# Sliding-window attention and a spectral mix on one core: attention by halves of the heads, mode weights by halves of the channels

## The chip, the core and the metric

The kernel runs on one core of a Trainium2 chip, as one launch. The metric is device time in microseconds from the launch's start to its end. The engines are PE (TensorE), DVE (VectorE), ACT (ScalarE), POOL (GpSimd) and SP (SyncE); the last two also issue the transfers here, POOL those that change the type from float32 to bfloat16 on the way, SP the others. Each engine takes its instructions in the order in which they stand in its queue.

## The reference

Attention with a causal window of 64 over 576 positions, for 8 batches and 8 heads of 64; the heads side by side are x (8 x 576 x 512). A real Fourier transform over the positions follows; of its frequencies the first 64 (the "modes") are each multiplied by a complex 512 x 512 matrix of their own, all others are set to zero; the inverse transform is added to x, and a dense layer with a ReLU is added to that.

```python
scores = scale * np.matmul(q, k.transpose(0, 1, 3, 2))
mask = (rel >= 0) & (rel < window)                    # window = 64
attn = softmax(where(mask, scores, -1e9)); x = heads side by side of (attn @ v)

X = np.fft.rfft(x, axis=1)
Xr, Xi = (np.real(X[:, :n_modes]), np.imag(X[:, :n_modes]))
Yr = np.einsum('bmd,mde->bme', Xr, w_r) - np.einsum('bmd,mde->bme', Xi, w_i)
Yi = np.einsum('bmd,mde->bme', Xr, w_i) + np.einsum('bmd,mde->bme', Xi, w_r)
Y[:, :n_modes] = Yr + 1j * Yi
u = x + np.fft.irfft(Y, n=S, axis=1)
return u + np.maximum(u @ w_ch, 0.0)
```

w_r and w_i are 64 matrices each of 512 x 512 float32, 1 MB a matrix, 134 MB in all. They are the bulk of what is read.

## The kernel before

**Attention** is written in 40 units (`units`), five for a batch: two for each half of the heads (4 heads, the positions 0 to 255 and 256 to 511), and one for the last 64 positions of both halves. A unit has 8 score tiles of 128 x 128 (the last 4): two heads of 64 rows by the 128 keys that the window can reach. One half of the heads of one batch is a group `g`; its q and k come as bfloat16 on 72 partitions (`load_qk`, POOL), its v as float32 (`load_v`, SP, rows of 256 bytes), which POOL casts (`cast_v`). `transpose_qk` turns q and k by 16 PE transposes and one ACT copy each, through the one PSUM bank of `ps_m`.

The order is written out by hand (`tc.manual_schedule()`), as a software pipeline over iterations `it`: for unit `it` PE subtracts the row maximum by a matmul (`do_sub`, L171) and ACT takes the exponential (`do_exp`, L179); for unit `it + 1` PE writes the mask and the scores (`do_s`, L144 to L158) and DVE takes the maximum (`do_max`, L165); for `it - 1` PE transposes the probabilities (`do_pt`, L186) and DVE copies them out (`do_ev`, L192); for `it - 2` PE multiplies by v (`do_pv`, L209) and DVE divides and writes `x_sb` (`do_norm`). The transposes of the next group stand between these. Once a batch is complete `do_dft` (L233) multiplies its x by the trigonometric table `trigF` in 20 matmuls into the bank of `ps_m`, and ACT copies the result into `XQ` (L235), with a negated copy of the imaginary part (L236). The columns of x that a DFT matmul takes are strided by four, so that the partition of `XQ` matches a load of the weights in which a partition reads four rows in one run of 8 KB.

Ahead of the loop come the masks and `trig_tables()`: a chain on DVE that ends in a Sin on ACT.

**The weights** come in 128 tiles (`wr` and `wi` of a mode) of 512 x 512, cast to bfloat16 by a POOL transfer (`load_weight`, L70), 512 KB each in SBUF, in a pool of 17. Seventeen are prefetched, spread over the 40 units. After attention the 64 modes follow in order: 8 matmuls of 16 columns x 512 for a mode (L404 and L406), a copy on ACT (L409), and two stores on SP (L410, L411) that gather the rows of `Yall`.

**The end**: the inverse table `trigI` is made (a chain of POOL, DVE and ACT, which the scheduler places into attention's last part); then for each batch and 128 positions one matmul gives the inverse transform (L425), DVE adds x (L428), PE transposes (L431), ACT copies (L435), four matmuls with `wch` follow (L438), and DVE and SP finish and store. The first of these matmuls needs all of `Yall`.

Of the kernel before, what the change touches and what calls it, by code (L numbers as in the profile page):

```python
# [13 lines left out]
ALU = mybir.AluOpType  # L14
# [3 lines left out]
W_BUFS = 17  # L18
# [6 lines left out]
def kernel(  # L25
# [15 lines left out]
    assert S == 576 and D == 64 and DM == 512 and H == 8  # L41
# [3 lines left out]
    NBLK = S // 64  # L45
    PSUM = bass.MemoryType.PSUM

    consts = ctx.enter_context(tc.tile_pool(name="consts", bufs=1))
# [10 lines left out]
    xpool = ctx.enter_context(tc.tile_pool(name="xpool", bufs=1))  # L59
    x_sb = xpool.tile([128, B, NTC, DM], BF16, name="x_sb")  # L60
    wch = xpool.tile([128, NDCH, DM], FP32R, name="wch")
    XQ = xpool.tile([128, NDCH, 3 * B, NM], BF16, name="XQ")
    Yall = xpool.tile([2 * NM, B, DM], BF16, name="Yall")
    wtpool = ctx.enter_context(tc.tile_pool(name="wtpool", bufs=W_BUFS))

    def load_weight(i):
        m, ri = divmod(i, 2)
        w = wtpool.tile([128, NDCH, DM], BF16, name="wi" if ri else "wr", tag="wt")
        src = moe_w_i if ri else moe_w_r
        nc.gpsimd.dma_start(out=w, in_=src[m].rearrange("(p c) e -> p c e", c=NDCH))  # L70
        return w

    wtiles = {}


    with ExitStack() as p1, tc.manual_schedule():
        rawp = p1.enter_context(tc.tile_pool(name="rawp", bufs=2))
        qtp = p1.enter_context(tc.tile_pool(name="qtp", bufs=3))
        vfp = p1.enter_context(tc.tile_pool(name="vfp", bufs=2))
        vdp = p1.enter_context(tc.tile_pool(name="vdp", bufs=1))  # L80
        ps_s = p1.enter_context(tc.tile_pool(name="ps_s", bufs=2, space=PSUM))
        ps_pt = p1.enter_context(tc.tile_pool(name="ps_pt", bufs=1, space=PSUM))
        ps_pv = p1.enter_context(tc.tile_pool(name="ps_pv", bufs=1, space=PSUM))
        ps_m = p1.enter_context(tc.tile_pool(name="ps_m", bufs=1, space=PSUM))

        NHB = 2 * B
        raws, qkT, vraw = {}, {}, {}

        def load_qk(g):
            b, hb = divmod(g, 2)  # L90
            for nm, src in (("k", k), ("q", q)):
                r = rawp.tile([72, 4, 8, D], BF16, name="raw" + nm, tag="raw" + nm)
                nc.gpsimd.dma_start(
                    out=r, in_=src[b, 4 * hb:4 * hb + 4].rearrange("h (p j) d -> p h j d", j=8))
                raws[g, nm] = r

        def load_v(g):
            b, hb = divmod(g, 2)
            vf = vfp.tile([128, NTC, 4, D], FP32, name="vf")
            vs = v[b, 4 * hb:4 * hb + 4]  # L100
            for c in range(4):
                nc.sync.dma_start(out=vf[:, c], in_=vs[:, c * 128:(c + 1) * 128, :].rearrange("h p d -> p h d"))
            nc.sync.dma_start(out=vf[0:64, 4], in_=vs[:, 512:576, :].rearrange("h p d -> p h d"))
            vraw[g] = vf
# [23 lines left out]
        for b in range(B):  # L128
            for hb in range(2):
                for cc in range(2):  # L130
                    tl = [(c2 * 4 + pr * 2 + par, 2 * b + hb, pr, 2 * (2 * cc + c2) + par)
                          for c2 in range(2) for pr in range(2) for par in range(2)]
                    units.append((b, hb, cc, tl))
            units.append((b, None, 2, [(hb * 2 + pr, 2 * b + hb, pr, 8) for hb in range(2) for pr in range(2)]))
        st = [dict() for _ in units]

        def do_s(u):
            b, hb, cc, tl = units[u]
            s = ps_s.tile([128, 8, 128], FP32, name="s")
            st[u]["s"] = s  # L140
            nb = len(tl) // 4
            for c2 in range(nb):
                mk = 2 if cc == 2 else (1 if (cc == 0 and c2 == 0) else 0)
                nc.tensor.matmul(out=s[:, 4 * c2:4 * c2 + 4, :], lhsT=ident_bf, rhs=mask_t[:, mk],  # L144
                                 start=True, stop=True)
            for t, g, pr, n in tl:
# [13 lines left out]

        def do_max(u):
            nt = len(units[u][3])
            mx = smp.tile([128, 8], FP32R, name="mx")
            st[u]["mx"] = mx
            nc.vector.tensor_reduce(out=mx[:, 0:nt], in_=st[u]["s"][:, 0:nt, :], axis=AX.X, op=ALU.max, negate=True)  # L165

        def do_sub(u):
            nt = len(units[u][3])
            s, mx = st[u]["s"], st[u]["mx"]
            for c2 in range(nt // 4):  # L170
                nc.tensor.matmul(out=s[:, 4 * c2:4 * c2 + 4, :], lhsT=ident_r,  # L171
                                 rhs=mx[:, 4 * c2:4 * c2 + 4].unsqueeze(2).to_broadcast([128, 4, 128]),
                                 start=False, stop=True, skip_group_check=True)

        def do_exp(u):
            nt = len(units[u][3])
            p = pp.tile([128, 8, 128], BF16, name="p")
            st[u]["p"] = p
            nc.scalar.activation(out=p[:, 0:nt, :], in_=st[u]["s"][:, 0:nt, :], func=ACT_F.Exp, scale=EX_SCALE)  # L179

        def do_pt(u):
            nt = len(units[u][3])
            pt = ps_pt.tile([128, 8, 128], BF16, name="pt")
            st[u]["pt"] = pt
            for t in range(nt):
                nc.tensor.transpose(out=pt[:, t, :], in_=st[u]["p"][:, t, :], identity=ident_bf)  # L186

        def do_ev(u):
            nt = len(units[u][3])
            ps = ptp.tile([128, 8, 128], BF16, name="pts")  # L190
            st[u]["ps"] = ps
            nc.vector.tensor_copy(out=ps[:, 0:nt, :], in_=st[u]["pt"][:, 0:nt, :])  # L192

        def do_pv(u):
            b, hb, cc, tl = units[u]
            o = ps_pv.tile([128, 2, 512], FP32, name="o")
            st[u]["o"] = o
            ps = st[u]["ps"]
            order = sorted(tl, key=lambda x: (x[0] // 4, x[2], x[3] % 2))
# [12 lines left out]

        def do_norm(u):
            b, hb, cc, tl = units[u]
            np_ = 128 if cc < 2 else 64
            o = st[u]["o"][0:np_, :, 0:260].rearrange("p c (h e) -> p c h e", e=65)
            r = smp.tile([128, 2, 4], FP32, name="r")
            nc.vector.reciprocal(out=r[0:np_].unsqueeze(3), in_=o[:, :, :, 64:65])
            rb = r[0:np_].unsqueeze(3).to_broadcast([np_, 2, 4, 64])
            if cc < 2:  # L220
                xo = x_sb[:, b, 2 * cc:2 * cc + 2, 256 * hb:256 * hb + 256]
                xo = xo.rearrange("p c (h d) -> p c h d", d=64)
            else:
                xo = x_sb[0:64, b, 4, :].rearrange("p (c h d) -> p c h d", c=2, d=64)
            nc.vector.tensor_tensor(out=xo, in0=o[:, :, :, 0:64], in1=rb, op=ALU.mult)  # L225
            st[u].clear()

        def do_dft(b):
            px = ps_m.tile([128, NDCH, 2 * NM], FP32, name="px", tag="misc")
            for dch in range(NDCH):  # L230
                for c in range(NTC):
                    nt = min(128, S - c * 128)
                    nc.tensor.matmul(out=px[:, dch, :], lhsT=x_sb[:nt, b, c, dch:DM:NDCH],  # L233
                                     rhs=trigF[:nt, c, :], start=(c == 0), stop=(c == NTC - 1))
            nc.scalar.copy(out=XQ[:, :, B + b:3 * B:B, :], in_=px.rearrange("p c (a m) -> p c a m", a=2))  # L235
            nc.scalar.mul(out=XQ[:, :, b, :], in_=px[:, :, NM:2 * NM], mul=-1.0)  # L236


        p0 = ExitStack()
        stmp = p0.enter_context(tc.tile_pool(name="stmp", bufs=1))  # L240
# [39 lines left out]
        nc.vector.tensor_copy(out=mask_t[:, 2, 1:4:2, :], in_=mask_t[:, 0, 0:4:2, :])  # L280

# [17 lines left out]
        p0.close()  # L299
        pp = p1.enter_context(tc.tile_pool(name="pp", bufs=2, reuse_waits="tile"))  # L300
        ptp = p1.enter_context(tc.tile_pool(name="ptp", bufs=2, reuse_waits="tile"))
        smp = p1.enter_context(tc.tile_pool(name="smp", bufs=3, reuse_waits="tile"))


        NU = len(units)

        def prep_for(u):

            b, hb, cc, tl = units[u]
            return 2 * b + hb if hb is not None and cc == 0 else None  # L310

        first = {}
        for u in range(NU):
            g = prep_for(u)
            if g is not None:
                first[g] = u

        tq = {}
        for g, u in first.items():
            grp = [("k", 0), ("q", 0), ("k", 1), ("q", 1)]  # L320
            for i, it in enumerate(grp):
                tq.setdefault(u - 3 + i // 2 if u else -3, []).append((g,) + it)
        npre = 0

        def prefetch(n):
            nonlocal npre
            for _ in range(n):
                if npre < W_BUFS:
                    wtiles[npre] = load_weight(npre)
                    npre += 1  # L330

        for it in range(-3, NU + 3):
# [3 lines left out]
            if 0 <= it < NU:  # L336
                do_sub(it)
                do_exp(it)
            if 0 <= it + 1 < NU:
                do_s(it + 1)  # L340
                do_max(it + 1)
            for x in todo[1:2]:
                transpose_qk(*x)
            if it >= 5 and it % 5 == 4:
                do_dft(it // 5 - 1)
            if 0 <= it - 1 < NU:
                do_pt(it - 1)
                do_ev(it - 1)
            if 0 <= it - 2 < NU:
                do_pv(it - 2)  # L350
                do_norm(it - 2)
# [3 lines left out]
            g = {u: g for g, u in first.items()}.get(it + 1)  # L355
            if g is not None and g + 2 < NHB:
                load_qk(g + 2)
                load_v(g + 2)
            if it >= 0:
                prefetch((it + 1) * W_BUFS // NU - npre)  # L360
            g = {u: g for g, u in first.items()}.get(it - 1)
            if g is not None and g + 1 < NHB:
                cast_v(g + 1)
            if it == 4:
# [110 lines left out]
```

## Time and profile before

| | |
|---|---|
| time, median of 3 runs | 555.59 us (554.82 to 560.37) |
| span of the profiled execution | 553.8 us |
| PE, DVE, ACT, POOL busy | 71%, 30%, 26%, 27% |
| share of the chain that ended last | DMA 53%, PE 32% |
| read from HBM, written | 163.58 MB, 9.44 MB |

The profiled execution's own time is its span and a little around it; the median of the runs lies 1.8 us above the span. A stretch's DMA share is the mean busy share of the 16 DMA engines, and goes above 1 where their packets overlap; its GB/s count what was written, for a casting load half of what was read. Busy PE time counts a matmul from start to modelled end, and matmuls overlap.

### The profile page before, as it was taken

The numbers are of one execution on the slowest core, as the hardware profiler recorded it, in microseconds if no ns is written. First come the engines' busy times: TensorE is split into PE (matmuls) and PEld (weight loads), VectorE is DVE, ScalarE is ACT, GpSimd is POOL, SyncE is SP. The second block draws the span as 40 slices with busy tenths as digits, with TensorE's granted clock in tenths as the row PEclk, the third lists the DMA queues.
The fourth block names the chain that finished last, engine by engine and source line by source line (L and its number), as shares of the span: only waits on it lengthen the run. The fifth ranks groups of instructions, "written<-read, shape, count | busy, mean of one in ns | idle before, by whom it ended". The sixth has DMA issues, their size and how long they took to land.

```text
span 553.8 us, 9433 instructions
## 1 busy us (share of the span) xinstructions
PE 391.0 (71%) x3896; PEld 207.8 (38%) x3896; DVE 168.3 (30%) x279; ACT 145.3 (26%) x222; POOL 150.0 (27%) x227
## 2 busy tenths in 40 slices
PE   0598899999997985556554655565475555699996
PEld 0366566666665441111111111121121111366664
DVE  5268176577569000000000000000000000287885
ACT  0465355556454130111011110111011011122221
POOL 7273474455532131222221222222121210000000
PEclk9999599999899798867788786778858888699999
DMA  9689999999964399999999999999999997034343
GB/s 155 103 144 228 163 161 200 191 180 206 176 130 78 55 216 215 214 214 215 214 215 214 215 214 215 214 215 213 214 215 214 214 214 155 7 139 143 133 138 129
DMA packets 77242, 98.14 MB, mean 177 GB/s; under 512 B 45456, under 2 KB 55696, under 8 KB 77200
## 3 DMA queue, kind: packets, MB, share of 16 engines
q0 software_dynamic: 31760, 77.62, 73.7%
q1 hardware_dynamic: 45440, 19.93, 15.0%
q8 instruction: 30, 0.49, 0.4%
q14 instruction: 12, 0.10, 0.1%
HBM read 163.58 MB, written 9.44 MB: 312 GB/s over the span
## 4 chain that ended last, share of the span: by engine, by line
DMA 53%; PE 32%; issue 6%; DVE 4%; POOL 3%; ACT 1%; SPq 0%; POOLq 0%; ACTq 0%
DMA wi<-in_moe_w_i_dram 48%; PE pout L438 7%; PE psut L431 4%; PE s L171 4%; PE px L233 3%; DVE mx L165 3%; DMA rawk<-in_k_dram 3%; PE tr L120 2%; PE s L144 2%; PE psy L425 2%; PE pt L186 2%; DMA vf<-in_v_dram 1%; PE o L209 1%; PE s L155 1%; PE s L152 1%
## 5 line engine op out<-in xcount | busy, mean ns | idle before, releaser
L406 PE MATMUL psm<-wi,XQ 128*16 128x512 bf16 x256 | 124.1, 486 | 99.2 <-DMA wi<-in_moe_w_i_dram 99.2
L404 PE MATMUL psm<-wr,XQ 128*16 128x512 bf16 x256 | 125.2, 490 | 20.0 <-DMA wr<-in_moe_w_r_dram 19.2
L428 DVE TENSOR_TENSOR ut<-x_sb,psy 128x512 f32<-128x512 bf16 (+1 forms) x40 | 27.1, 683 | 298.4 <-PE psy L425 297.0
L409 ACT CAST stg<-psm 16x512 bf16<-16x512 f32 x64 | 36.8, 575 | 253.5 <-PE psm L406 249.7
L404 PEld LDWEIGHTS <-XQ 128*16 128x16 bf16 x256 | 29.1, 114 | 191.6 <-issue 134.8
L70 POOL DMA_DIRECT2D wi<-in_moe_w_i_dram x64 | 34.2, 534 | 123.4 <-DMA wi<-in_moe_w_i_dram 94.3
L70 POOL DMA_DIRECT2D wr<-in_moe_w_r_dram x64 | 34.2, 535 | 102.2 <-DMA wr<-in_moe_w_r_dram 54.3
L165 DVE TENSOR_REDUCE mx<-s 128x8 fp32r<-128x1024 f32 (+1 forms) x40 | 44.7, 1117 | 41.2 <-PE s L152 40.0
L406 PEld LDWEIGHTS <-XQ 128*16 128x16 bf16 x256 | 31.0, 121 | 41.0 <-issue 27.4
L438 PE MATMUL pout<-wch,utt 128*128 128x512 f32 (+1 forms) x160 | 44.1, 414 | 0.5 <-ACT utt L435 0.5
L179 ACT ACTIVATE p<-s 128x1024 bf16<-128x1024 f32 (+1 forms) x40 | 37.6, 940 | 17.4 <-PE s L171 15.8
L435 ACT CAST utt<-psut 128x512 fp32r<-128x512 f32 (+1 forms) x33 | 19.1, 580 | 54.5 <-PE psut L431 54.5
L442 DVE SCALAR_TENSOR_TENSOR ot<-pout,ut 128x512 f32<-128x512 f32 (+1 forms) x40 | 27.5, 687 | 14.8 <-PE pout L438 14.8
L171 PE MATMUL s<-mx,ident_r 128*128 128x512 f32 x72 | 28.1, 465 | 5.0 <-DVE mx L165 4.2
L192 DVE COPY pts<-pt 128x1024 bf16<-128x1024 bf16 (+1 forms) x40 | 25.3, 632 | 20.0 <-PE pt L186 20.0
L438 PEld LDWEIGHTS pout<-wch,utt 128*128 128x128 f32 (+1 forms) x160 | 26.8, 181 | 10.5 <-ACT utt L435 3.1
L225 DVE TENSOR_TENSOR x_sb<-o,r 128x512 bf16<-128x512 f32 (+1 forms) x40 | 27.6, 689 | 1.2
L123 ACT COPY kT<-tr 128x576 bf16<-128x576 bf16 x32 | 20.4, 638 | 27.1 <-PE tr L120 27.1
L120 PE MATMUL tr<-ident_bf,rawk 72*64 72x72 bf16 x512 | 16.3, 210 | 14.1 <-DMA rawk<-in_k_dram 11.0
L144 PE MATMUL s<-mask_t,ident_bf 128*128 128x512 bf16 x72 | 24.7, 419 | 0.0
L123 ACT COPY qT<-tr 128x576 bf16<-128x576 bf16 x32 | 20.5, 639 | 15.7 <-PE tr L120 15.7
L431 PE MATMUL psut<-ident,ut 128*128 128x128 f32 (+1 forms) x160 | 24.4, 274 | 0.2
(81 smaller groups left out, 424.8 us busy)
## 6 DMA issues: line engine op xcount, KB each, us to landing
wr<-in_moe_w_r_dram POOLq DMA_DIRECT2D x64, 512.0 KB, 19.6
wi<-in_moe_w_i_dram POOLq DMA_DIRECT2D x64, 512.0 KB, 19.6
vf<-in_v_dram SPq DMA_DIRECT2D x64, 128.0 KB
out_dram<-ot SPq DMA_DIRECT2D x32, 256.0 KB
rawk<-in_k_dram POOLq DMA_DIRECT2D x16, 288.0 KB, 7.6
rawq<-in_q_dram POOLq DMA_DIRECT2D x16, 288.0 KB, 8.0
Yall<-stg SPq DMA_DIRECT2D x128, 8.0 KB
vf<-in_v_dram SPq DMA_DIRECT2D x16, 64.0 KB
```

What stands on the lines that cost most here:

```text
L70: nc.gpsimd.dma_start(out=w, in_=src[m].rearrange("(p c) e -> p c e", c=NDCH))
L123: nc.scalar.copy(out=t.rearrange("p (n j) -> p n j", j=8), in_=pt.rearrange("p j n -> p n j"))
L144: nc.tensor.matmul(out=s[:, 4 * c2:4 * c2 + 4, :], lhsT=ident_bf, rhs=mask_t[:, mk], start=True, stop=True)
L165: nc.vector.tensor_reduce(out=mx[:, 0:nt], in_=st[u]["s"][:, 0:nt, :], axis=AX.X, op=ALU.max, negate=True)
L171: nc.tensor.matmul(out=s[:, 4 * c2:4 * c2 + 4, :], lhsT=ident_r, rhs=mx[:, 4 * c2:4 * c2 + 4].unsqueeze(2).to_broadcast([128, 4, 128]), st ...
L179: nc.scalar.activation(out=p[:, 0:nt, :], in_=st[u]["s"][:, 0:nt, :], func=ACT_F.Exp, scale=EX_SCALE)
L225: nc.vector.tensor_tensor(out=xo, in0=o[:, :, :, 0:64], in1=rb, op=ALU.mult)
L404: nc.tensor.matmul(out=psm[:, :], lhsT=XQ[:, dch, B:3 * B, m], rhs=wr[:, dch, :], start=(dch == 0), stop=False)
L406: nc.tensor.matmul(out=psm[:, :], lhsT=XQ[:, dch, 0:2 * B, m], rhs=wi[:, dch, :], start=False, stop=(dch == NDCH - 1))
L409: nc.any.tensor_copy(out=stg[:, :], in_=psm[:, :])
L431: nc.tensor.transpose(out=psut[:, ech * nt:(ech + 1) * nt], in_=ut[:nt, ech * 128:(ech + 1) * 128], identity=ident[:nt, :nt])
L438: nc.tensor.matmul(out=pout[:nt, :], lhsT=utt[:, ech * nt:(ech + 1) * nt], rhs=wch[:, ech, :], start=(ech == 0), stop=(ech == NDCH - 1))
```

## The change

- Attention goes over the halves of the heads first: groups 0 to 7 are the first four heads of all batches, groups 8 to 15 the last four. The units keep their sizes; the unit of the last 64 positions is now two batches of one half. `do_dft` is called for each group (its 256 channels), 16 times for 8.
- Two modes share a tile. A weight tile now holds 256 rows of the matrices of modes 2p and 2p + 1, on partitions 0 to 63 and 64 to 127: two loads of 64 partitions each, again four rows in a run of 8 KB. `XQ` becomes block-diagonal (the columns of the other mode are zero), so that 4 matmuls with 32 columns do for the tile; there are still 512 in all. `XQ0` is zeroed on DVE before `trig_tables()`, `XQ1` on POOL in the loop; the unused rows of x_sb are zeroed on DVE too.
- Four pairs of modes share a PSUM tile, 32 partitions each, written by matmuls to different column groups; `mode_step` takes two pairs in turns.
- Weights stream under attention: 19 tiles are paced over the first 24 units, then `early_step` runs a mode step on the first half of the channels in every second unit, ten in all (20 pairs), each of which from the third on issues 4 more tiles. Their sums are kept in `Yacc`. After attention the memory of its pools takes 12 more slots (`ring2`); the pairs 20 to 31 do both halves, then pairs 0 to 19 the second half. wch is loaded after attention, not in it.
- `finish_group` sums and rounds on DVE and issues 16 stores on SP for a group of eight modes (two for each mode, as before).
- The scores' PSUM tile is one bank (three of them) for two (two of them): mask, scores, maximum, subtraction and exponential go by halves of a unit.
- The DFT becomes 40 matmuls of 64 columns for each group, to the upper and lower half of the partitions in turns, and six ACT copies.
- The inverse table's pool stands where `ring2` was.

```diff
-W_BUFS = 17
+RING = 11
+FIRST = 8
...
+    XQ = {0: xpool.tile([128, NJ, NPAIR, 3, 2, B], BF16, name="XQ0")}
+    ring = pool("ring", bufs=RING, side="right")
+    wave = pool("wave", bufs=FIRST, side="right")
...
+    EARLY = 5
+    order = [(p, 0) for p in range(4 * EARLY)]
+    for grp in range(EARLY, NGRP):
+        for p2 in (4 * grp, 4 * grp + 2):
+            order += [(p2, 0), (p2 + 1, 0), (p2, 1), (p2 + 1, 1)]
+    for grp in range(EARLY):
+        order += [(p, 1) for p in range(4 * grp, 4 * grp + 4)]
...
+    def load_weights(n):
...
+            w = (wave if nload < FIRST else ring).tile(
+                [128, NJ, DM], BF16, name="wi" if ri else "wr", tag="wt")
+            src = moe_w_i if ri else moe_w_r
+            for mi in range(2):
+                nc.gpsimd.dma_start(
+                    out=w[64 * mi:64 * mi + 64],
+                    in_=src[2 * p + mi, HALF * hb:HALF * hb + HALF, :].rearrange("(p j) e -> p j e", j=NJ))
...
+    def mode_step(psm, pairs, hb, first, last):
+        n = 2 * NJ
+        for i in range(n):
+            ri, j = divmod(i, NJ)
+            for p in pairs:
+                g = p % 4
+                nc.tensor.matmul(out=psm[32 * g:32 * g + 32, :],
+                                 lhsT=XQ[hb][:, j, p, 1 - ri:3 - ri].rearrange("k t a b -> k (t a b)"),
+                                 rhs=wtiles[p, hb, ri][:, j, :],
+                                 start=(first and i == 0), stop=(last and i == n - 1),
+                                 tile_position=(0, 32 * g))
...
         def load_qk(g):
-            b, hb = divmod(g, 2)
+            hb, b = divmod(g, B)
...
+        def do_s(u, c2):
...
+            s = ps_s.tile([128, 4, 128], FP32, name="s")
...
+            mx = smp.tile([128, 4], FP32R, name="mx")
+            st[u]["mx", c2] = mx
+            nc.vector.tensor_reduce(out=mx, in_=s, axis=AX.X, op=ALU.max, negate=True)
...
+            for c2 in range(nh):
+                s, mx = st[u]["s", c2], st[u]["mx", c2]
+                nc.tensor.matmul(out=s, lhsT=ident_r, rhs=mx.unsqueeze(2).to_broadcast([128, 4, 128]),
+                                 start=False, stop=True, skip_group_check=True)
+                nc.scalar.activation(out=p[:, 4 * c2:4 * c2 + 4, :], in_=s, func=ACT_F.Exp, scale=EX_SCALE)
...
+        def do_dft(g):
+            hb, b = divmod(g, B)
+            px = ps_m.tile([128, NJ, 2, NPAIR], FP32, name="px", tag="misc")
+            for j in range(NJ):
                 for c in range(NTC):
...
+                    for mi in range(2):
+                        nc.tensor.matmul(out=px[64 * mi:64 * mi + 64, j],
+                                         lhsT=x_sb[:, b, c, HALF * hb + j:HALF * hb + HALF:NJ],
+                                         rhs=trigF[:, c, :].rearrange("p (a m i) -> p a m i", a=2, i=2)[:, :, :, mi],
+                                         start=(c == 0), stop=(c == NTC - 1))
...
+            for mi in range(2):
+                ro = slice(64 * mi, 64 * mi + 64)
+                for t in range(2):
+                    nc.scalar.copy(out=XQ[hb][ro, :, :, 1 + t, mi, b], in_=px[ro, :, t, :])
+                nc.scalar.mul(out=XQ[hb][ro, :, :, 0, mi, b], in_=px[ro, :, 1, :], mul=-1.0)
+
+        def zero_xq(hb, eng):
+            for mi in range(2):
+                eng.memset(XQ[hb][64 * mi:64 * mi + 64, :, :, :, 1 - mi, :], 0.0)
...
+        nc.vector.memset(x_sb[64:128, :, 4, :], 0.0)
+        zero_xq(0, nc.vector)
...
+        NA = NU // 2 + 4
...
+        def early_step():
...
+            ps_ = [4 * grp + 2 * q2, 4 * grp + 2 * q2 + 1]
+            mode_step(psm, ps_, 0, first=True, last=True)
+            load_weights(4 if step >= FIRST // 4 else 0)
+            if step == FIRST // 4 - 1:
+                close(wave)
...
+                zero_xq(1, nc.gpsimd)
...
+            if q2 == 1:
+                nc.scalar.copy(out=late["Yacc"][:, grp, :], in_=psm)
+            step += 1
...
+            if it >= 7 and it % 5 in (2, 3):
+                do_dft(2 * (it // 5 - 1) + it % 5 - 2)
...
+            if 0 <= it < NA:
+                load_weights((it + 1) * (FIRST + RING) // NA - nload)
...
+            if it >= NA and (it - NA) % 2 == 0 and step < 2 * EARLY:
+                early_step()
...
+        ring2 = pool("ring2", bufs=12, reuse_waits="tile")
...
+        nc.gpsimd.dma_start(out=wch, in_=moe_w_ch.rearrange("(c p) e -> p c e", p=128))
...
+        def finish_group(grp, psm):
+            stg = stgpool.tile([128, DM], BF16, name="stg")
+            if grp < EARLY:
+                nc.vector.tensor_tensor(out=stg, in0=psm, in1=late["Yacc"][:, grp, :], op=ALU.add)
+            else:
+                nc.vector.tensor_copy(out=stg, in_=psm)
+            for g in range(4):
+                for mi in range(2):
+                    m, r0 = 8 * grp + 2 * g + mi, 32 * g + 8 * mi
+                    nc.sync.dma_start(out=late["Yall"][m:m + 1, :, :], in_=stg[r0:r0 + B, :])
+                    nc.sync.dma_start(out=late["Yall"][NM + m:NM + m + 1, :, :], in_=stg[r0 + 2 * B:r0 + 3 * B, :])
...
+        ring_, ring = ring, ring2
+        load_weights(12)
...
+        for i, (grp, q2, hb, f, l) in enumerate(late_steps):
+            if q2 == 0 and f:
+                psm = ps_mc.tile([128, DM], FP32, name="psm")
+            mode_step(psm, [4 * grp + 2 * q2, 4 * grp + 2 * q2 + 1], hb, f, l)
+            ring = ring_ if nload % 8 < 4 else ring2
+            load_weights(4)
+            if q2 == 1 and l:
+                finish_group(grp, psm)
...
-            nc.any.tensor_copy(out=stg[:, :], in_=psm[:, :])
-            nc.sync.dma_start(out=Yall[m:m + 1, :, :], in_=stg[0:B, :])
-            nc.sync.dma_start(out=Yall[NM + m:NM + m + 1, :, :], in_=stg[B:2 * B, :])
```

## The prediction

> **What bounds the kernel now.** I read the page's slices first, then busy time by stretches cut where the slices change, then the groups by form, the chain of work, and the timeline of one attention period. The stretches (us; busy time of each engine with its count; granted clock, DMA share, GB/s written):
>
> ```profile
> 13.00:35.00 22.00, 13.98 (x254) 9.06 (x253) 6.92 (x7) 10.64 (x14) 9.68 (x12) 1.00 0.63 101
> 35.00:83.00 48.00, 42.48 (x896) 29.29 (x891) 29.90 (x49) 24.23 (x35) 26.11 (x31) 0.86 1.05 187
> 83.00:160.00 77.00, 71.49 (x1528) 50.01 (x1528) 50.96 (x81) 42.60 (x61) 41.47 (x48) 0.98 1.11 189
> 160.00:195.00 35.00, 30.09 (x377) 17.74 (x377) 17.87 (x38) 12.86 (x19) 8.63 (x14) 0.90 0.39 72
> 195.00:471.70 276.70, 158.19 (x468) 52.02 (x466) 0.00 (x0) 33.93 (x59) 54.87 (x104) 0.80 1.05 211
> 471.70:484.00 12.30, 8.87 (x30) 5.12 (x30) 2.78 (x5) 1.75 (x3) 0.00 (x0) 0.58 0.01 3
> 484.00:553.80 69.80, 65.21 (x339) 43.91 (x337) 52.94 (x83) 17.97 (x31) 0.00 (x0) 1.00 0.39 136
> ```
>
> The reader is to see three regimes. From 195 to 471.7 the DMA engines are full and PE waits: weights alone set the pace. 214.5 GB/s (the slices) is 524 KB in 2.444 us a tile, and 111 of the 128 tiles come here. From 83 to 160 PE is busy 93% and the DMA share is no lower (1.11): the DMA is nearly full under attention too. The DMA idles only at 13 to 35 and 160 to 195. So moving weights under attention can win those gaps and no more. The output stage (484 on) is PE's and stays.
>
> ```profile
> L165 DVE TENSOR_REDUCE mx<-s 128x8 fp32r<-128x1024 f32 x32 | 39.2, 1224 | 40.0 <-PE s L152 40.0
> ...
> L209 PE MATMUL o<-vd,pts 128*64 128x65 bf16 x576 | 18.3, 200 | 1.7 <-DVE x_sb L225 1.7
> ...
> L235 ACT CAST XQ<-px 128x512 bf16<-128x512 f32 x8 | 4.7, 586 | 20.4 <-PE px L233 20.4
> ...
> L165 DVE TENSOR_REDUCE mx<-s 128x4 fp32r<-128x512 f32 x8 | 5.5, 690 | 1.3 <-PE s L158 1.3
> ...
> L236 ACT ACTIVATE XQ<-px 128x256 bf16<-128x256 f32 x8 | 3.1, 389 | 0.0
> ...
> L278 DVE MEMSET mask_t<- 128x128 bf16 x1 | 0.2, 165 | 0.1
> ```
>
> These are the rows that price the added instructions. One period of attention (a batch, five units) runs from 106.07 to 124.23, 18.2 us. PE streams in all of it but 0.85 us before the DFT:
>
> ```profile
> 118.51 0.61 PE L144 MATMUL s<-mask_t,ident_bf 128*128 128x512 bf16 x2
> ...
> 120.07 0.64 ACT L123 COPY qT<-tr 128x576 bf16<-128x576 bf16 x1 [0.64 <-PE tr L120]
> ...
> 120.76 2.13 PE L233 MATMUL px<-trigF,x_sb 128*128 128x128 bf16 x20 [0.73 <-ACT qT L123]
> ...
> 122.82 0.62 PE L186 MATMUL pt<-ident_bf,p 128*128 128x128 bf16 x8
> ...
> 123.37 0.45 PE L209 MATMUL o<-vd,pts 128*64 128x65 bf16 x16
> ```
>
> **The DMA's ledger.** A period moves two half-head groups of q, k and v and 2.125 weight tiles, so a group costs (18.2 - 2.125 x 2.444) / 2 = 6.5 us of DMA time. Sixteen groups are 104 us, 128 tiles 313, wch (1 MB read) 2.4: 419 us. The last tile lands at 471.7, so some 52 us are idle.
>
> **Part 1, the start.** Two kinds of zero fill go on VectorE ahead of the trig tables: 8 x 512 elements of x_sb and 2 x 3072 of XQ0, 10240 in all. Bounds: from L278 with a 134 ns start (the one-column rows of VectorE) (165 - 134)/128 = 0.24 ns an element, 2.9 us; with no start 1.29 ns, 13.2 us. I take VectorE's slope between its two max sizes, (1224 - 690)/512 = 1.04 ns: 10.7 us, as a fill without a source is nearest to an element-by-element row. Two us hide in VectorE's wait for Bft at 6.6 to 8.6. The other 8.6 delay the Sin on ScalarE, and behind it in ScalarE's queue the first kT copy (16.1 before): all of attention. The first subtraction of the max goes from 25.6 to 34.2. The Trainium skill ("VectorE: DVE Perf Modes", "Zero memsets can be issued as uint32 (trn2)") says a memset takes a cycle an element whatever the type, unless zeros are issued as 4-byte words; by the first the fill is the 10.7 us taken, by the second half of it, an end 5.3 us sooner.
>
> **Part 2, attention's pace.** Split scores: per unit two more changes between the 64-row tiles and the whole array. Two masks stream 0.43 us and the scores start 0.54 after the first (118.51 to 119.05), so a change costs 0.11; four full units a period make 0.9 us. The maxima become 2 x 0.69 for 1.22 and the exps 2 x 0.60 for 1.02; VectorE and ScalarE have room (51 and 43 of 77 us), and three score banks let the second half wait only for the first exp. Without DFT and its wait a unit is then (18.2 - 0.85 - 2.06 + 0.9)/5 = 3.23 us.
>
> The DFT goes from one per batch to two, each 40 matmuls of 64 columns for 20 of 128. Now each takes 106 ns; PV's 64-column loads start every (0.45 - 0.20)/15 = 17 ns, the two column halves overlapping. Bounds 0.7 and 4.2 us a DFT. The stationary columns are still strided by four, which costs this DFT twice the contiguous transposes (pt: 56 ns), so twice PV's rate, some 42 ns: 1.7 us. Around it: 0.65 us for the qT copy, as psum bank "misc" is shared, and its eviction in six ScalarE pieces. Two points (512 in 586, 256 in 389) give 0.19 + 0.77 ns an element, 0.29 us for 128, so 1.85 us with the signal, of which pt and PV cover 0.9. The next unit's first transpose waits 0.95, with scores, exps and the mode step behind it in PE's order. A DFT thus costs 1.7 + 0.65 + 0.95 = 3.3 us.
>
> **Part 3, weights under attention.** Nineteen tiles are paced over 24 units, then a mode step of 16 matmuls (4 tiles) every second unit, ten in all; from the third on each issues 4 tiles. Two matmuls of 512 columns go to different column groups: 16 x 0.21 = 3.4 us if serial, 1.7 if overlapped as PV's are; I take 2.0. GpSimd waits in each for PE to free the slots, with the q/k loads and V's cast queued behind; they are needed two units later, so the wait is covered.
>
> Each tile becomes two loads of 64 partitions. Issue is 0.53 us each (L70), 4.3 us for a step's eight against 10 us of transfer, covered. The transfer: at best the present 2.444. At worst the nearest row of part-filled loads, q and k on 72 partitions: V's packets are what is left of the hardware queue (15.0% of the span less 27 for the output and about 3 for Yall, 53 us, 3.3 a group), a group has (0.53 + 1.18 + 1.23) x 5 / 2 = 7.35 in the first load of two (the DMA shares of the first three stretches of 5 us), so q and k have 4.05, at share 1.2 3.4 us for 590 KB, that is 3.0 us a tile. With packets and source runs as now I take 2.50, near the low end. The Trainium skill speaks against the halving: "DMA: Bandwidth & Descriptors", "Rules for kernel authors" says not to split a transfer by partition halves, since they serialize; "SBUF — State Buffer", "Door 1: The DMA port swizzle" gives 64 partitions 8 of 16 ports, 218 GB/s at the limit and 196 measured. By 218 a tile is an estimated 2.41 us and nothing changes; by 196 it is 2.68, and the end some 19 us later.
>
> **The sum.** Unit 28, where the third step's issue begins: 34.2 + 28 x 3.23 + nine DFTs x 3.3 + 2 steps x 2.0 + 7 us of starting stalls (nine units took 34.5 us to 60 where 3.05 each would be 27.4) = 165. The DMA's need until then (12 groups and 19 tiles from 28 on, 126 us) fits. From there on it stays full: 2 us to fill, two groups 13, wch 2.4, 109 tiles x 2.50 = 272.5. PE is done with attention at about 235 (12 units, three iterations of drain, 8 steps, 70 us), with a backlog queued; in the late part at least 7 tiles stay outstanding when the alternating rings wait. The late matmuls (16 a step, under 7 us even at half clock) hide behind 10 us of tiles. Last landing 165 + 2 + 13 + 2.4 + 272.5 = 455 for 471.7.
>
> **The tail.** From the last landing to the end is 553.8 - 471.7 = 82.1 us. The last group now stores 16 pieces of Yall on SP where the last mode stored 2:
>
> ```profile
> 475.05 0.63 SPq L410 DMA_DIRECT2D Yall<-stg  x1
> 475.73 0.64 SPq L411 DMA_DIRECT2D Yall<-stg  x1
> ...
> 477.78 1.44 PE L425 MATMUL psy<-Yall,trigI 128*128 128x512 bf16 x3 [3.41 <-DMA Yall<-stg]
> ```
>
> At 0.68 apart, 14 more are 9.5 us, and psy waits for all; the sum on VectorE for the ScalarE copy is 0.1. The inverse table (6.8 us from iota to trigI by its rows, now behind the late tiles' memory) hides under those stores; without them it would show. Tail 91.7. Span 455 + 91.7 = 546.7 for the profiled 553.8; the median is 555.6, 1.8 above the span, so 548.5, told as 548.
>
> **The rivals.** (a) Slower, the half-partition loads: at 3.0 us a tile 109 x 0.5 = 54.5 us later, 603; halfway, 576. It decides from 2.565 us a tile. For it: every remaining tile pays it, with the DMA as the bound. Against: 4 KB packets stay, and now no port is shown full. (b) Slower, attention's pace: DFT pieces at 106 ns and evictions of 0.39 give 3.1 more a DFT, 28 us by unit 28: 577; it decides from 4.1 us a DFT for 3.3. (c) Better: fills at 0.24 ns and tiles at 2.444: 7.7 + 6.1 less, 535. (d) It doesn't do what it says: if GpSimd's waits let no tile in before 235, 235 + 2 + 2.4 + 272.5 + 91.7 + 1.8 = 605; against it, eleven ring slots are freed four by four.
>
> **Numbers.** Forecast 0.50, (a) 0.19, (b) 0.12, (c) 0.16, (d) 0.03. About 1% can be told from no change, that is 550 and 561. The forecast's own range, 538 to 560, lies across the first: faster 0.31, same 0.11, slower 0.08. With (c) all faster, (a) 0.01, 0.02, 0.16, (b) 0, 0.01, 0.11 and (d) slower: 0.48, 0.14, 0.38. The range is from (c) with 4 us to spare, 531, to (a) at 2.81 a tile, 582.
>
> **What would show it.** First kT copy near 24.7; fills of some 10 us on VectorE; px 40 pieces in 1.7 us, then six evictions of 0.29; DMA share over 1.0 without a gap from about 165 to 455; tiles 2.50 apart; 16 stores 0.68 apart ahead of psy. Wrong would be a late stage not bound by the DMA, a tile over 2.57, or a first psy later than 480 (471 is expected).

## The result, and the profile after

The change made the kernel slower: **591.06 us** (median of 4 runs, 586.91 to 594.46) against 556.39 (median of 4), a ratio of **1.0653, 95% interval 1.0586 to 1.072**. The forecast was 548, in a range of 531 to 582. The profiled execution has a span of 585.1 us for 553.8; it belongs to the lowest of the four runs, so its stretches account for 31 of the 35 us between the medians.

The busy time by stretches, cut where the stages change (us; busy time of each engine in the order PE, PEld, DVE, ACT, POOL, each with its count; then the granted clock, the DMA share, and GB/s written):

```profile
13.00:35.00 22.00, 13.61 (x191) 8.71 (x192) 8.05 (x14) 9.19 (x14) 7.00 (x10) 1.00 0.75 108
35.00:83.00 48.00, 38.60 (x771) 28.04 (x776) 24.77 (x46) 27.50 (x46) 25.16 (x35) 0.82 1.04 178
83.00:160.00 77.00, 56.17 (x1136) 42.63 (x1144) 34.05 (x62) 47.84 (x79) 36.88 (x48) 0.78 0.94 162
160.00:195.00 35.00, 29.59 (x508) 19.45 (x511) 13.24 (x24) 18.69 (x33) 15.51 (x15) 0.80 0.35 64
...
300.00:400.00 100.00, 41.41 (x160) 11.14 (x160) 2.07 (x3) 0.00 (x0) 40.72 (x79) 0.60 1.07 213
...
495.00:510.00 15.00, 0.58 (x1) 0.28 (x3) 1.29 (x3) 0.76 (x2) 0.00 (x0) 0.50 0.04 9
510.00:585.10 75.10, 69.33 (x353) 47.48 (x357) 55.56 (x87) 19.13 (x33) 0.00 (x0) 0.98 0.36 127
```

The stretch from 83 to 160 says most. PE was busy 71.5 of its 77 us and is busy 56.2 now, at a granted clock of 0.78 for 0.98, and the DMA share fell from 1.11 to 0.94: attention got slower and the weights did not get in under it. From 160 to 195, the gap that the change was to fill, the share is 0.35, where it was 0.39. The late pace, 213 GB/s, is the old one. And from 495 to 510 little runs but the 16 stores.

The groups that answer to those that priced the change (by form):

```profile
L282 ACT CAST XQ<-px 64x128 bf16<-64x128 f32 x64 | 43.6, 943 | 26.6 <-PE px L275 26.4
...
L283 ACT ACTIVATE XQ<-px 64x128 bf16<-64x128 f32 x32 | 36.1, 1127 | 0.0
...
L216 DVE TENSOR_REDUCE mx<-s 128x4 fp32r<-128x512 f32 x72 | 49.8, 691 | 100.8 <-PE s L206 74.0 <-PE s L212 26.3
...
L250 PE MATMUL o<-vd,pts 128*64 128x65 bf16 x576 | 20.2, 211 | 0.8 <-issue 0.8
```

The halved maxima and PV are what they were priced at. **The eviction is not:** a piece of 128 elements was put at 0.29 us and takes 0.94 and 1.13, 96 pieces 79.7 us of ACT in sum of their lengths, where the whole eviction took 7.8 before (pieces overlap in part, as the next view shows). What follows from it, in the timeline of one period:

```profile
115.13 1.40 PE L275 MATMUL px<-trigF,x_sb 128*64 128x64 bf16 x40
...
116.56 1.36 ACT L282 CAST XQ<-px 64x128 bf16<-64x128 f32 x2 [1.49 <-PE px L275]
...
117.40 1.13 ACT L283 ACTIVATE XQ<-px 64x128 bf16<-64x128 f32 x1
...
118.54 1.36 ACT L282 CAST XQ<-px 64x128 bf16<-64x128 f32 x2
...
119.39 1.12 ACT L283 ACTIVATE XQ<-px 64x128 bf16<-64x128 f32 x1
120.56 0.69 PE L174 MATMUL tr<-ident_bf,rawk 72*64 72x72 bf16 x16 [3.10 <-ACT XQ L283]
...
121.18 1.22 PE L224 MATMUL s<-mx,ident_r 128*128 128x512 f32 x2
```

Six pieces run from 116.56 to 120.51, 3.95 us. The next transposes of k need the same PSUM bank, and PE, which takes its queue in order, stands still for 3.10 us. It then runs at half clock for a while: the granted clock is 1.00 up to 119.5 and 0.50 from 120 to 137, and these 16 transposes take 0.69 us (those of q at 113.94, before the wait, 0.45), the subtraction 1.22 (0.70 at 112.72). In the columns of the stretches above:

```profile
112.00:119.50 7.50, 5.40 (x135) 4.22 (x133) 4.60 (x9) 5.16 (x10) 6.86 (x9) 1.00 0.98 176
120.00:137.00 17.00, 12.47 (x210) 9.60 (x211) 5.07 (x9) 9.31 (x15) 3.18 (x6) 0.50 0.94 161
```

From this DFT to the one at 145.09, a period of five units, it is 30.0 us (the two periods before it took 30.2 and 28.3); it was 18.2. In the list of waits up to 250 us this is PE's largest:

```profile
PE tr L174 <- ACT XQ L283: 28.0, 11, 3.1
PE tr L174 <- DMA rawk<-in_k_dram: 12.3, 2, 7.0
```

(us in all, times, longest.) And the end, from the last mode matmul, which is over at 489.1:

```profile
489.18 0.15 DVE L478 TENSOR_SCALAR Gph<-Gcol 128x1 f32<-128x1 f32 x1 [19.87 <-PE psm L120]
...
495.09 0.68 ACT L488 ACTIVATE Ti<-Qi 128x576 f32<-128x576 f32 x1
495.81 0.52 DVE L493 TENSOR_SCALAR trigI<-Ti,coef 128x576 bf16<-128x576 f32 x1 [2.15 <-ACT Ti L488]
496.24 0.68 DVE L441 TENSOR_TENSOR stg<-psm,Yacc 128x512 bf16<-128x512 f32 x1
496.95 0.63 SPq L447 DMA_DIRECT2D Yall<-stg  x1
...
507.15 0.64 SPq L448 DMA_DIRECT2D Yall<-stg  x1
...
509.21 0.58 PE L507 MATMUL psy<-Yall,trigI 128*128 128x512 bf16 x1 [20.12 <-DMA Yall<-stg]
```

The last sum (L441) stands in DVE's queue behind the inverse table's whole chain, 7 us, and only then come the 16 stores. The table does not lie under the stores, it lies ahead of them.

### The profile page after: what moved, and what is told of

It reads as the page before. It is cut to its first block, busy times and chain, and to the rows that moved or that the text cites. A ratio compares the mean times of both kernels' runs of the same rounds, so it can differ in the third digit from the quotient of the medians.

```text
span 585.1 us, 10420 instructions
## 1 busy us (share of the span) xinstructions
PE 356.2 (61%) x4348; PEld 208.9 (36%) x4376; DVE 183.7 (31%) x322; ACT 168.2 (29%) x275; POOL 219.5 (38%) x357
## 4 chain that ended last, share of the span: by engine, by line
DMA 43%; PE 33%; ACT 11%; issue 5%; DVE 4%; POOL 2%; SPq 2%; POOLq 0%; DVEq 0%; ACTq 0%
DMA wr<-in_moe_w_r_dram 22%; DMA wi<-in_moe_w_i_dram 19%; PE pout L520 6%; ACT XQ L282 5%; PE tr L174 5%; PE s L224 4%; PE psut L513 3%; PE px L275 3%; ACT XQ L283 2%; DMA rawk<-in_k_dram 2%; PE pt L232 2%; PE s L198 2%; PE s L209 2%; PE psy L507 2%; ACT qT L177 1%
## 5 line engine op out<-in xcount | busy, mean ns | idle before, releaser
L120 PE MATMUL psm<-wr,XQ 128*32 128x512 bf16 x256 | 64.4, 553 | 113.0 <-DMA wr<-in_moe_w_r_dram 112.1
L120 PEld LDWEIGHTS <-XQ 128*32 128x32 bf16 x512 | 31.8, 118 | 205.7 <-DMA wr<-in_moe_w_r_dram 129.3
L107 POOL DMA_DIRECT2D wi<-in_moe_w_i_dram x128 | 66.6, 523 | 85.7 <-DMA wi<-in_moe_w_i_dram 55.9
L107 POOL DMA_DIRECT2D wr<-in_moe_w_r_dram x128 | 66.6, 524 | 75.2 <-DMA wr<-in_moe_w_r_dram 53.9
L216 DVE TENSOR_REDUCE mx<-s 128x4 fp32r<-128x512 f32 x72 | 49.8, 691 | 100.8 <-PE s L206 74.0
L120 PE MATMUL psm<-wi,XQ 128*32 128x512 bf16 x256 | 63.4, 537 | 17.3 <-DMA wi<-in_moe_w_i_dram 17.3
L282 ACT CAST XQ<-px 64x128 bf16<-64x128 f32 x64 | 43.6, 943 | 26.6 <-PE px L275 26.4
L226 ACT ACTIVATE p<-s 128x512 bf16<-128x512 f32 x72 | 39.8, 600 | 13.7 <-PE s L224 12.0
L283 ACT ACTIVATE XQ<-px 64x128 bf16<-64x128 f32 x32 | 36.1, 1127 | 0.0
L209 PE MATMUL s<-kT,qT 64*64 64x64 bf16 x320 | 27.7, 219 | 5.8 <-issue 5.8
```

The costliest lines, as they stand in the source:

```text
L107: nc.gpsimd.dma_start(out=w[64 * mi:64 * mi + 64], in_=src[2 * p + mi, HALF * hb:HALF * hb + HALF, :].rearrange("(p j) e -> p j e", j=NJ))
L120: nc.tensor.matmul(out=psm[32 * g:32 * g + 32, :], lhsT=XQ[hb][:, j, p, 1 - ri:3 - ri].rearrange("k t a b -> k (t a b)"), rhs=wtiles[p, hb ...
L209: nc.tensor.matmul(out=s[ro, t, 0:64], lhsT=lq, rhs=kT[ro, 64 * n:64 * n + 64], start=False, stop=True, skip_group_check=True)
L216: nc.vector.tensor_reduce(out=mx, in_=s, axis=AX.X, op=ALU.max, negate=True)
L226: nc.scalar.activation(out=p[:, 4 * c2:4 * c2 + 4, :], in_=s, func=ACT_F.Exp, scale=EX_SCALE)
L282: nc.scalar.copy(out=XQ[hb][ro, :, :, 1 + t, mi, b], in_=px[ro, :, t, :])
```

## The experiments

The theory after the profile: most of the loss is the form in which ACT writes `XQ`. In the kernel after, neighbours in a piece lie 48 elements (96 bytes) apart, since the pair of modes was made the outer index; in the kernel before they lay side by side. Its rivals: the half-partition loads, the split of the DFT as such, the order of the tail.

**The pairs innermost** (e1_xq_inner: the kernel after with `XQ` laid out so that a piece writes runs of 32 elements; the matmuls' stationary columns are strided instead):

```diff
-    XQ = {0: xpool.tile([128, NJ, NPAIR, 3, 2, B], BF16, name="XQ0")}
+    XQ = {0: xpool.tile([128, NJ, 3, 2, B, NPAIR], BF16, name="XQ0")}
...
-                                 lhsT=XQ[hb][:, j, p, 1 - ri:3 - ri].rearrange("k t a b -> k (t a b)"),
+                                 lhsT=XQ[hb][:, j, 1 - ri:3 - ri, :, :, p].rearrange("k t a b -> k (t a b)"),
...
-                    nc.scalar.copy(out=XQ[hb][ro, :, :, 1 + t, mi, b], in_=px[ro, :, t, :])
+                    nc.scalar.copy(out=XQ[hb][ro, :, 1 + t, mi, b, :], in_=px[ro, :, t, :])
...
```

> The changed kernel with XQ laid out with the pairs of modes innermost, so that ScalarE writes runs of 32 elements where it wrote single elements 96 bytes apart; the matmuls take their 32 columns 64 bytes apart. Theory A (the strided eviction sets the pace of attention): the pieces fall from 0.94 and 1.13 us to about 0.3, a DFT block loses some 2.1 us on ScalarE and about 1.3 of PE at half clock, the first mode step starts near 142 instead of 165, the last tile lands near 462 instead of 487, and the time is about 565. Theory B (the split scores, the DFT in 40 pieces and the clock set the pace): the pieces get short too, but the first mode step stays within 5 us of 165 and the time within 586 to 592. Theory C (GpSimd's queue and the loads under attention set it): the first mode step comes early, but attention still ends near 255 and the time stays over 582.

Measured: 565.12 us, 1.0162 of the kernel before on the same chip (1.0112 to 1.0211). The groups, and the stretch of attention after its DFTs have begun:

```profile
L282 ACT CAST XQ<-px 64x128 bf16<-64x128 f32 x64 | 13.5, 259 | 32.0 <-PE px L275 31.9
...
L283 ACT ACTIVATE XQ<-px 64x128 bf16<-64x128 f32 x32 | 8.9, 278 | 0.0
```

```profile
83.00:142.00 59.00, 49.90 (x1080) 36.29 (x1080) 31.25 (x57) 30.52 (x77) 31.58 (x41) 0.88 1.06 187
```

With runs of 32 a piece takes 0.26 and 0.28 us, near the 0.29 of the forecast, and the six of a DFT 1.21 us (113.92 to 115.13) for 3.95. Nothing else in the arithmetic changed, and 27 of the 36 us of loss are gone (the ratio falls by 0.049 of 556). The first mode step comes at 142.3 us for 164.9, with eight DFTs ahead of it, so 2.8 us each; the third at 163.5 for 191.3, with nine whole evictions ahead of it, so 3.1 each. PE's waits for the eviction fall from 28.0 us to 2.9. The matmuls' stationary columns, now 64 bytes apart, cost nothing that the late stage would show, since the DMA bounds it. The clock is not all the eviction's: with its waits gone the stretch still has 0.88 for the 0.98 of the kernel before.

**The same stride in the kernel before** (e3_before_strided: modes outside, the 24 columns inside, elements 48 bytes apart):

```diff
-    XQ = xpool.tile([128, NDCH, 3 * B, NM], BF16, name="XQ")
+    XQ = xpool.tile([128, NDCH, NM, 3 * B], BF16, name="XQ")
...
-            nc.scalar.mul(out=XQ[:, :, b, :], in_=px[:, :, NM:2 * NM], mul=-1.0)
+            nc.scalar.mul(out=XQ[:, :, :, b], in_=px[:, :, NM:2 * NM], mul=-1.0)
...
```

> The kernel before with one part of the change alone: XQ with the modes outside and the batches inside, so that ScalarE's two copies of a DFT write single elements 48 bytes apart. Theory A (a ScalarE write of single 2-byte elements far apart costs 5 to 7 ns an element): 512 elements take some 3.2 us for 0.59 and 256 some 1.6 for 0.39, a batch is 3 to 4 us longer, attention ends 25 to 30 us later, and as the stream starts with it the time is about 583. Rival (the slow copies of the changed kernel come from their 64 partitions or their small size): both copies stay under 0.7 us and the time within 1% of 556.

Measured: 584.82 us, 1.0512 (1.0468 to 1.0555), and in the groups the rows that were 586 and 389 ns:

```profile
L235 ACT CAST XQ<-px 128x512 bf16<-128x512 f32 x8 | 20.0, 2505 | 19.8 <-PE px L233 19.8
...
L236 ACT ACTIVATE XQ<-px 128x256 bf16<-128x256 f32 x8 | 13.5, 1689 | 0.0
```

The index order alone, put into the old kernel, loses 28 us: the first mode matmul comes at 214.9 us for 184.5. Taken out of the new one it gives 27 back. That is the cause from both sides, for the greater part of the loss. By the length of an instruction, with the 0.19 us start that the two old rows give, an element costs an estimated (2505 - 190) / 512 = 4.5 ns in the copy and (1689 - 190) / 256 = 5.9 in the negation at 48 bytes, and 5.9 and 7.3 ns at the 96 bytes of the change, for 0.77 side by side. The instructions overlap in part, so what PE waits for is the whole eviction of a DFT: 3.68 us here (112.95 to 116.63) for 0.87 in the kernel before (122.93 to 123.80).

**Every load of the kernel before in halves** (e4_before_split), which is the mechanism of rival (a) by itself:

```diff
-        nc.gpsimd.dma_start(out=w, in_=src[m].rearrange("(p c) e -> p c e", c=NDCH))
+        for mi in range(2):
+            nc.gpsimd.dma_start(out=w[64 * mi:64 * mi + 64],
+                                in_=src[m, 256 * mi:256 * mi + 256, :].rearrange("(p c) e -> p c e", c=NDCH))
```

> The kernel before with one part of the change alone: each tile of weights comes as two loads of 64 partitions. If a half load costs what the q and k loads do (3.0 us a tile), 111 tiles make 617; at the 196 GB/s that the Trainium skill gives 64 partitions (2.68 us) it is 582; at the pace that the changed kernel's late part shows (2.46) it is 558, no change.

Measured: 568.0 us, 1.0203 (1.0147 to 1.026). The stretches of attention and of the stream:

```profile
83.00:160.00 77.00, 66.93 (x1320) 45.68 (x1314) 43.27 (x70) 36.49 (x53) 39.44 (x51) 0.89 1.12 172
300.00:400.00 100.00, 55.55 (x158) 17.41 (x156) 0.00 (x0) 11.48 (x20) 40.28 (x79) 0.80 1.06 212
```

The stream runs at 212 GB/s, 524.3 KB / 212 = 2.47 us a tile for 2.444: the halves are hardly slower there, and 111 tiles at 0.03 are 3 us. But the time is 11 us worse, and most of it is lost before the stream: the first mode matmul comes at 198.2 us for 184.5. That is not the pace of a tile. Two more runs separate the stream from attention.

**Only the 111 tiles of the stream in halves** (e7_split_late), and **only the 17 prefetched ones** (e10_split_early); the edit is the one above for a part of the tiles, shown for the first; the second turns the condition round.

```diff
-        nc.gpsimd.dma_start(out=w, in_=src[m].rearrange("(p c) e -> p c e", c=NDCH))
+        if i < W_BUFS:
+            nc.gpsimd.dma_start(out=w, in_=src[m].rearrange("(p c) e -> p c e", c=NDCH))
+            return w
+        for mi in range(2):
...
```

> The kernel before with the loads of 64 partitions only for the 111 tiles after attention; the 17 prefetched ones stay whole. The kernel with all of them split was 11.5 us longer, with 2.46 us a tile in the stream for 2.44. If the cost lies in attention (twice the issues on GpSimd ahead of the q and k loads, PE delayed), the time is 557 to 559. If it lies in the stream it stays at 566 to 568.

> The kernel before with the loads of 64 partitions only for the 17 tiles prefetched under attention. All tiles split cost 11.5 us, the 111 late ones alone some 3 to 4. If the two add up, this one costs 7 to 8 us, in attention: 562 to 563. If the 11.5 came from chance placement (PE's waits for nothing that the profile shows), it is within 1% of before, 555 to 558.

Measured: 558.49 us, 1.0058 (1.0019 to 1.0097), first mode matmul at 184.4; and 560.84 us, 1.0116 (1.0062 to 1.0171), first mode matmul at 190.4. The second lies between the two outcomes that were named for it (562 to 563, and 555 to 558). So the halves cost some 3 us in the stream and 6 under attention, together 9.7 by the ratios where e4 lost 11.3; the intervals hold the difference. Why 17 split loads cost attention 6 us stays open: in e4 PE's longest waits from 83 to 160 are put down to "issue" (2.0, 1.5 and 1.4 us), which names no engine and no transfer. And e4 and e10 issue the same loads under attention, yet their profiled executions (one of each) differ by 7.8 us at the first mode matmul, so that stretch can differ from one execution to another by more than the 6 us.

**The inverse table ahead of the late stage** (e2_trig_early: the block of the table moved, unchanged, to just before `ring2`, in memory of its own; the strided eviction stays):

```diff
+        stmp2 = pool("stmp2")
+        MtI = stmp2.tile([128, S], FP32, name="MtI")
...
+        nc.vector.tensor_scalar(out=trigI, in0=Ti, scalar1=coef, scalar2=None, op0=ALU.mult)
+
         ring2 = pool("ring2", bufs=12, reuse_waits="tile")
```

> The changed kernel with the inverse table made after attention, ahead of the late loads, in a pool of its own, not after the last late step. Theory A (VectorE does the table ahead of the last sum, so 16 stores start 7 us late): the sum starts 0.5 us after the last matmul instead of 7.5, the time is 7 us less, about 584. Rival (the tail is the 16 stores alone, or the table delays the late loads by as much): no change, 589 to 593.

Measured: 584.45 us, 1.0493 (1.0439 to 1.0546), 9 us of ratio better than the change. In the timeline the sum now follows the last matmul, which is over at 494.1, at once, and the first store at 494.81:

```profile
494.09 0.69 DVE L464 TENSOR_TENSOR stg<-psm,Yacc 128x512 bf16<-128x512 f32 x1 [19.86 <-PE psm L120]
```

From the last matmul to the first psy it is 13.1 us for 20.1, 7.0 less. The two spans differ only by 2.4 us because this execution's last tile came 5 us later, 3 of them there already at its first mode step (167.9 for 164.9), ahead of the table; the medians, 6.6 apart, bear the 7.0 out.

**Three mends together** (e5_three_mends: e1, e2, and the second store of each mode on ACT's queue):

```diff
-                    nc.sync.dma_start(out=late["Yall"][NM + m:NM + m + 1, :, :], in_=stg[r0 + 2 * B:r0 + 3 * B, :])
+                    nc.scalar.dma_start(out=late["Yall"][NM + m:NM + m + 1, :, :], in_=stg[r0 + 2 * B:r0 + 3 * B, :])
```

> The changed kernel with three mends together: the XQ layout with the pairs innermost (565.1 by itself), the inverse table ahead of the late loads (6.6 us by itself), and the 16 last stores shared by SP's and ScalarE's queues. If the pieces are independent: 565.1 - 6.6 - 8 x 0.68 = 553, half a per cent under the kernel before. Rival (the two queues do not issue side by side): the stores of the last group still take 10 us and the time is 558. Rival (earlier table and layout overlap in what they gain): over 560.

Measured: 553.36 us, 0.9952 of the kernel before (0.9914 to 0.999). The two queues issue side by side:

```profile
463.60 5.82 SPq L470 DMA_DIRECT2D Yall<-stg  x8
463.60 5.44 ACTq L471 DMA_DIRECT2D Yall<-stg  x8
```

Eight on each take 5.8 us where 16 on SP took 10.8; psy begins 8.2 us after the last matmul for 20.1. The 7.0 of e2 and these 5.0 agree with the 11.7 us by which its ratio lies below that of e1 (0.021 of 556).

**The weights' loads spread** (e6_spread: e5, and each early step issues two tiles at once and two an iteration later), to get q and k out from behind four tiles' loads in POOL's queue:

```diff
-            load_weights(4 if step >= FIRST // 4 else 0)
+            load_weights(2 if step >= FIRST // 4 else 0)
+            late["owed"] = 2 if step >= FIRST // 4 else 0
...
+            elif it > NA:
+                load_weights(late.pop("owed", 0))
...
```

> The same three mends, and each early step issues two tiles at once and two an iteration later, where it issued four at once. If the q and k loads wait behind a burst of eight half tiles (rawk landing in 13 us, PE waiting 19 us for it in all), rawk's longest landing falls to about 8 us and the time by 3 to 6 us. If the DMA is full from the third step on anyhow, PE's waits get shorter but the last tile lands within 2 us of where it did, and the time is the same.

Measured: 552.47 us, 0.9949 (0.9911 to 0.9987), the same as e5: the first theory missed, its rival held. The longest landing of a k load did not fall (13.5 us, 11.7 in e5), PE's waits for k went from 14.1 to 11.3 us, and the last tile landed no earlier. Halving the burst did not bring q and k in earlier; what delays them stays open.

**The sums by halves** (e9_halves: e6, and the sum and the stores of a group of eight modes go by halves, each four modes as soon as their last step is done, so that 8 stores are left at the end):

```diff
-            if q2 == 1 and l:
-                finish_group(grp, psm)
+            if l:
+                finish_half(grp, q2, psm)
```

> The three mends with the loads spread, and each group of modes summed and stored in two halves, after each of its two last steps, so that 8 stores are left after the last step, on two queues: 4 x 0.68 = 2.7 us less than the run with 16 on two queues (552.5), so 550, 0.8% under the kernel before. Rival: VectorE's reading of one half of the bank holds up the matmuls of the other half, or the last landing of Yall comes as late: no change, 552 to 553.

Measured: **549.93 us, 0.9898 (0.9854 to 0.9942)**: 1% under the kernel before, with an interval clear of no change, and 7% below the change. From the last matmul, over at 469.4, to psy at 474.68 it is 5.3 us, 2.9 less than in e5 and e6 (8.2), which is the 2.7 expected; the time by itself does not tell e9 from e6, whose intervals overlap. This version beats both kernels.

## Why the prediction was wrong, step by step

The span was put at 546.7 and was 585.1, 38.4 more. By the landmarks of the sum: the third step 26.3 later (191.3 for 165), from there to the last landing 6.2 more (296.2 for 290), the tail 5.9 longer (97.6 for 91.7).

- **The failed step: "0.29 us for 128"**, the eviction in Part 2. The two old rows were read as a law in the number of elements, but they hold for runs side by side, and the diff changed the order of the indices of `XQ` with the shape. A DFT was put at 3.3 us; the period of 30.0 for 22.7 makes it (30.0 - 22.7) / 2 = 3.65 more, nine of them 33 us by the third step, less 7 for a cheaper start: the 26. e1 takes 2.8 (up to the first mode step) to 3.1 (up to the third) of it back at each DFT; the rest, about half a microsecond each, is not the eviction's. A piece took 0.94 to 1.13 us for 0.29, and the six of a DFT, which overlap in part, 3.95 us for 1.85; what hung on them (a PE wait of up to 3.10 us for 0.95, then half clock) followed. Its upper end was 0.39, in rival (b), though the added operation writes at another stride than the rows that priced it.
- A page bears on it. The Trainium skill, "SBUF — State Buffer", "Specifications (TRN2)", states that SBUF has lines of 16 bytes, and that full bandwidth needs at least two hits on a line. Elements 48 and 96 bytes apart never share one. The runs agree in direction: 4.5 to 7.3 ns an element for 0.77, by the estimate above.
- **Rival (b) named the right place for the wrong reason.** Its threshold, 4.1 us a DFT, was passed, and its price, 3.1 more a DFT, happens to be the one that e1 gives (2.8 to 3.1). But it put most of that into matmuls at 106 ns: the 40 took 1.41 us (predicted 1.7), and the evictions, whose pieces it put at 0.39, made it. That its price came out is luck.
- **The start** was priced 7 us too high: the zero fills were put at 10.7 us and took 4.4, so the first subtraction came at 26.9 for 34.2 (25.6 before). Nearly 2 us more came from the chain behind them, which took 5.1 us (12.26 to 17.33) for 6.8 before (8.62 to 15.43). In the timeline of DVE:

```profile
7.07 1.76 DVE L330 MEMSET x_sb<- 64x2048 uint32 x1 [0.47 <-issue]
9.19 1.34 DVE L287 MEMSET XQ<- 64x1536 uint32 x1 [0.36 <-issue]
```

- They are issued as 4-byte words, which is the exception that the Trainium skill, "VectorE: DVE Perf Modes", "Zero memsets can be issued as uint32 (trn2)", states; (1760 - 1340) / 512 is 0.82 ns a word, 0.41 an element. The row that the prediction preferred was the wrong one, and its error hid part of the other: without it the third step would have been some 33 us late.
- **"From there on it stays full"** failed too, by 6.2 us, though the tiles at 2.46 us for 2.50 gave some 4 back. The slices of 10 us that fall short are 190 to 200 with 106 GB/s and 230 to 240 with 183, where a full one has some 206. In both POOL first waits for PE to finish a mode step and free the slots: 7.29 us until 192.78, and 5.96 until 234.71. In e1 the same stage has its hole from 210 to 230 (138 GB/s, about 7 us lost), with another wait, in POOL's list:

```profile
POOL vd L165 <- DMA vf<-in_v_dram: 31.1, 7, 10.6
```

- A load of V issued on SP at 192.57 landed at 218.2, while weights streamed; POOL's cast waited 10.6 us for it, and the next weight loads stand behind the cast in POOL's queue. The prediction had named that queue and called its waits covered. Why this load took 25.6 us was not tested.
- **The tail:** 16 stores 0.68 apart, right to the digit; **"hides under those stores"**, wrong. The table's chain and the last sum are both on DVE, and the chain stands first. e2 priced it: 7.0 us.
- **Right:** the late pace, 2.46 us a tile for 2.50, and rival (a) falls with it. The Trainium skill, "SBUF — State Buffer", "Door 1: The DMA port swizzle", gives 64 partitions 218 GB/s at the limit and 196 as measured; the halves streamed at 212 to 213 where whole tiles streamed at 214.5, so no run here shows a lower pace for 64 partitions, and the 2.68 us a tile of the second were not seen. The mode step of 16 matmuls took 1.9 us at full clock (174.34 to 176.24), for 2.0 predicted and 3.4 if serial: pairs on different column groups do overlap.
- **Rival (c)** had the fills nearly right (4.4 us for 2.9) and the tiles not (2.46 for 2.444). With the evictions as priced (e1) the span is still 563.3, 16.6 over the forecast: the third step 1.5 us earlier, then 11.0 lost in the stream (about 7 in the hole above; the rest was not traced) and 7.1 in the tail. So even without the stride the change as made stays 1.6% slower than before.

## What to carry to other kernels

A row prices an instruction in its form, and the form includes the step between the elements that it writes: where a diff reorders the indices of a tensor, read the innermost step of every access to it, and bound the cost if no row has that step. An eviction that shares a PSUM bank with the next stage is on PE's path, less what PE does meanwhile (3.95 us made a wait of 3.10 here, 1.21 one of 0.37), so it is worth more than its engine's busy share says (ACT was busy 62% of the stretch that it bounded). And a chain that "hides" under a transfer must stand in its engine's queue behind the instruction that starts that transfer, not ahead of it.

## What was not expected of the hardware

- ACT's 2-byte writes at steps of 48 and 96 bytes cost an estimated 4.5 to 7.3 ns an element for 0.77 side by side, by the length of an instruction; the whole eviction of a DFT, whose instructions overlap, took 3.68 us for 0.87 at 48 bytes (e3) and 3.95 for 1.21 at 96 (e1).
- A stop of PE costs more than its length. Of the ten stops of 2.1 to 3.1 us at the eviction two fell into a stretch at half clock; at each of the other eight the granted clock, read in slices of 0.5 us, fell to 0.50 within 1.5 us of the stop's end and stayed there for 3.5 to 17 us (the transposes took 0.69 us for 0.45, the subtraction 1.22 for 0.70). The mean from 83 to 160 was 0.78 for 0.98.
- POOL's casting loads land as if some eight were outstanding at most, whatever their size, an estimate from the median landing times: 9.6 us for 256 KB pieces (7.8 x 1.23), 19.6 for 512 KB ones (8 x 2.444). Halving the loads halves what is queued; the late stage stood it, POOL waiting 55.9 and 53.9 us for its own loads with the stream full.
- Splitting 17 prefetched loads by partitions cost some 6 us, in attention, and 111 in the stream about 3. Only the second is explained, by the pace.
